# Attention backward on one core: which unit of a group hands a product to GpSimd, and where turned dK, dV and dQ are placed

## The chip, the cores and the metric

The kernel runs on one NeuronCore of a Trainium2 chip. The core has five engines with their own instruction queues: TensorE (PE, with weight loads shown as PEld), VectorE (DVE), ScalarE (ACT), GpSimd (POOL) and SyncE (SP, which issues DMAs). Every queue is worked off in order; engines wait for each other on semaphores. The metric is the device time of one execution in microseconds (us), taken as the median over several runs.

## The reference

The reference is one transformer layer with adaptive layer norm, forward and backward: 2048 tokens of width 512, 32 heads of width 16, and a squared-ReLU MLP of width 1792. It returns the layer's output and the gradients of all inputs but one. What matters here is the backward pass through the attention:

```python
scores = jnp.einsum('bhqd,bhkd->bhqk', q, k) * scale
p = _softmax(scores, axis=-1)
o = jnp.einsum('bhqk,bhkd->bhqd', p, v)
...
_out, _vjp = jax.vjp(_f, A_x, A_wqkv, A_wo, B_w1, B_b1, B_w2, B_b2, c, w_mod)
_grads = _vjp(grad_out)
```

With P = exp(scores), unnormalised, and dO already divided by the softmax sums, the backward pass is: dP = dO V^T minus the row term, dS = P * dP, dV = P^T dO, dK = dS^T Q, dQ = dS K. The row term rides along in two extra rows of the matmul that makes dP, so the only elementwise work on a tile of dP is one product with P.

## The kernel before

The kernel has three parts in time: the forward pass with the MLP forward and backward mixed into it (to about 1172 us), the attention backward loop `attn_bwd` (to about 2416 us), and a last part with the weight gradients of the projection and the gradient of x. The change lies in `attn_bwd` alone.

**Loops.** The 32 heads are taken two at a time: 8 quads `g` times 2 pairs `jp` give 16 passes, called pairs here. Within a pair, `c` runs over 4 chunks of 512 keys and `ib` over 16 blocks of 128 queries. One (c, ib) is a unit: a tile of 128 queries by 512 keys for both heads of the pair (`a` = 0, 1). There are 1024 units. Four units with neighbouring `ib` form a group; a pair has 16 groups, numbered here 0 to 15 as `4*c + ib//4`. Within a group the unit's number is `i`.

**A step.** For each unit the loop body issues, in program order:

1. at `i == 2`, one waiting entry of `turnq`, if there is one (line 1578; see below);
2. for each head: the score matmul of this unit (L1584, into a tile of the PSUM pool `stp`), the matmul dP of the unit before (L1509, in `dP`, into a tile of the PSUM pool `dpp`) with its product dS = dP * P on VectorE (L1513), and then exp on ScalarE (L1587), which writes P into `pu`;
3. the entry of the unit before into the lists `pend` and, at the end of a group, the DMA transpose of the group's dS from SP (L1530, in `dS`);
4. in odd steps the matmuls of dK and dV for two earlier units (`kv_two`, L1455), in even steps those of dQ from dS transposed two to three groups earlier (`dq`, L1478);
5. at `i == 2`, `turn_ds`.

So the product of unit i falls in step i + 1: step 1 of a group makes dP and dS of unit 0, step 2 those of unit 1, and unit 3 is finished in step 0 of the next group. The two pools `stp` and `dpp` have three buffers each, so a matmul into either waits until the tile three places earlier has been read. The score and dP matmuls of a head use different halves of the array's rows and run side by side.

**Two kinds of groups.** `off(c, ib)` is true for the groups with odd numbers. In these, called thinned groups here, one of VectorE's eight products is left out: for unit 0, head 1, `dP` returns the tile, and `dP_pool` has ScalarE copy it to an SBUF tile (L1521, `junk6` or `csq` in turn) and GpSimd multiply it with P (L1522). The call stands after the exponential of head 1 in the same step. All 32 blocks of these groups' dS are transposed by DMA. In the even groups VectorE makes all eight products, and `turn_ds` transposes 4 of the 32 blocks on TensorE (L1543), which ScalarE copies out (L1544); the DMA transposes the other 28.

**dK, dV and dQ.** dK and dV of a chunk gather in one PSUM bank over 16 units; after the last of them, which falls in step 3 of the next even group, ScalarE copies the bank to `kvT` (L1458). These are [rows of the head, keys] and must be turned: `turn` transposes 8 blocks on TensorE (L1468) into a tile of `stp`, and ScalarE copies the parts out (L1472, two copies). A pair's dQ gathers in `accq`, is scaled by VectorE into `dqT` (L1483), and turned by `turn_q` (four transposes, L1491; one copy, L1492). Finished pieces wait in `turnq`, and one is taken per group. In 15 of the 16 pairs, groups 1 and 2 turn halves of the pair before's dK and dV, and group 3 turns its dQ.

**Order.** The order on TensorE, SP and GpSimd is that of the program in this loop. ScalarE and VectorE are ordered by the framework's planner; in the trace their order in this loop is that of the program too. GpSimd also issues the loads of the next pair's operands (L1573), each after a one-element copy (`tick`, L1572) that ties it to the product of unit 0, head 0 of the group before.

Of the kernel before, what the change touches and what calls it, by code (L numbers as in the profile page):

```python
# [105 lines left out]
class K:  # L106
# [1322 lines left out]
    def attn_bwd(self):  # L1429
# [17 lines left out]
        pend, pendq, turnq = [], [], []  # L1447
# [12 lines left out]
        def turn(g, jp, kvT, s0):  # L1460

            if kvT is None:
                return turn_q(g, jp)
            h0 = 4 * g + 2 * jp
            n = ST // 2
            tp = stp.tile([P, n, P], BF16, name="st")
            for st in range(n):
                nc.tensor.transpose(tp[:, st, :], kvT[:, (s0 + st) * P:(s0 + st + 1) * P], self.ident[:])  # L1468
            v = tp[:].rearrange("p s (t a e) -> p t s a e", t=2, a=2)
            for t, dst in enumerate((self.dk_t, self.dv_t)):  # L1470
                d = dst[:, s0:s0 + n, h0 * DH:(h0 + 2) * DH].rearrange("p s (a d) -> p s a d", a=2)
                nc.scalar.copy(d, v[:, t, :, :, 0:DH])  # L1472

        def dq(u):
            (T, g, jp, c, ib0, a, sub, dsT) = u
            col = 32 * (2 * jp + a) - DH * a
            for i in range(G):
                nc.tensor.matmul(accq[32 * i:32 * i + 32, ib0 // G, :], lhsT=T["K"][:, 4 * c + sub, col:col + 32],  # L1478
                                 rhs=dsT[:, (i * 2 + a) * 4 + sub, :],
                                 start=(c == 0 and ib0 == 0 and a == 0 and sub == 0), stop=False,  # L1480
                                 skip_group_check=True)
            if (c, ib0, a, sub) == (SC - 1, ST - G, 1, 3):
                nc.vector.tensor_scalar(self.dqT[:], accq[:].rearrange("p b q -> p (b q)"), self.scale, None, ALU.mult)  # L1483
                turnq.append((g, jp, None, 0))
# [9 lines left out]
        def kv_two(n=2):  # L1494
            for u in pend[2 - n:2]:
                kv(u)
            (T, g, jp, c, ib, kvT, pu, ds) = pend[1]
            del pend[:2]
            if c % 2 and ib == ST - 1 and (g, jp) == (NQ - 1, 1):
                turnq.append((g, jp, kvT, 4 * (c - 1)))  # L1500
            elif c == SC - 1 and ib == ST - 1:
                turnq.extend((g, jp, kvT, s0) for s0 in (0, ST // 2))

        def dP(u, a):

            (T, g, jp, c, ib, kvT, pu, dsg, i, grp) = u
            rd = slice(64 - 64 * jp, 128 - 64 * jp)
            dp = dpp.tile([P, 512], F32, name="dp")
            nc.tensor.matmul(dp[:], lhsT=T["dOT"][rd, ib * P:(ib + 1) * P],  # L1509
                             rhs=masked["VT"][a][rd, 512 * c:512 * (c + 1)], start=True, stop=True)  # L1510
            if a == 1 and i == 0 and off(c, ib):
                return dp
            nc.vector.tensor_tensor(dsg[:, i, a], dp[:], pu[:, a, :], ALU.mult)  # L1513

        def off(c, ib):
            return (c * SC + ib // G) % 2 == 1

        def dP_pool(u, dp):
            (T, g, jp, c, ib, kvT, pu, dsg, i, grp) = u
            f = (self.junk6, self.csq)[(c * SC + ib // G) // 2 % 2]  # L1520
            nc.scalar.copy(f[:], dp[:])  # L1521
            nc.gpsimd.tensor_tensor(dsg[:, i, 1], f[:], pu[:, 1, :], ALU.mult)  # L1522

        def dS(u):

            (T, g, jp, c, ib, kvT, pu, dsg, i, grp) = u
            pend.append((T, g, jp, c, ib, kvT, pu, dsg[:, i]))
            if i == G - 1:
                dsT, n = grp
                nc.sync.dma_start_transpose(dsT[:, n:, :], dsg[:].rearrange("p i a k -> p (i a k)")[:, n * P:])  # L1530
                for a in range(2):
                    for sub in range(4):
                        pendq.append((T, g, jp, c, ib - G + 1, a, sub, dsT))

        def turn_ds(dsg, grp, skip):

            dsT = dtp.tile([P, 8 * G, P], BF16, name="dsT")
            grp.extend((dsT, 0 if skip else 4))
            if skip:
                return  # L1540
            tp = stp.tile([P, 4, P], BF16, name="st")
            for b in range(4):
                nc.tensor.transpose(tp[:, b, :], dsg[:, 0, 0, b * P:(b + 1) * P], self.ident[:])  # L1543
            nc.scalar.copy(dsT[:, 0:4, :], tp[:])  # L1544
# [4 lines left out]
        for g in range(NQ):  # L1549
            for jp in range(2):  # L1550
                if jp == 0:
                    if g + 1 < NQ:
                        Tn, later = self.load_group(g + 1)
                    else:
                        Tn, later = None, self.wq_pieces(1) + self.load_wmt()
                    cut = len(later) // 2 if Tn else len(later)
                    pieces = self.pair_pieces(g, 1) + later[:cut]
                    later = later[cut:]
                elif g + 1 < NQ:
                    pieces = self.pair_pieces(g + 1, 0) + later  # L1560
                else:
                    pieces = [(self.xhat1_6[:, st, :], self.xhat1_d.rearrange("(st p) d -> p st d", p=P)[:, st, :])
                              for st in range(ST)]
                kvT = kvp.tile([P, S], BF16, name="kvT")
                total = len(pieces)
                for c in range(SC):
                    c0 = 512 * c
                    for ib0 in range(0, ST, G):
                        m = c * (ST // G) + ib0 // G
                        while pieces and (total - len(pieces)) * SC * ST <= m * G * total:  # L1570
                            if last:
                                nc.gpsimd.tensor_copy(tick[:], last[7][0:1, 0, 0, 0:1])  # L1572
                            nc.gpsimd.dma_start(*pieces.pop(0))  # L1573
                        dsg, grp = self.dsp.tile([P, G, 2, 512], BF16, name="ds"), []
                        for i in range(G):
                            ib = ib0 + i
                            q = slice(ib * P, (ib + 1) * P)
                            if turnq and i == 2:
                                turn(*turnq.pop(0))
                            pu = self.pup.tile([P, 2, 512], BF16, name="pu")  # L1580
                            for a in range(2):
                                stt = stp.tile([P, 512], F32, name="st")
                                rs = slice(64 * jp, 64 * jp + 64)
                                nc.tensor.matmul(stt[:], lhsT=T["QT"][rs, q], rhs=masked["KT"][a][rs, c0:c0 + 512],  # L1584
                                                 start=True, stop=True)
                                held = dP(last, a) if last else None
                                nc.scalar.activation(pu[:, a, :], stt[:], ACT.Exp, scale=self.scale)  # L1587
                                if held is not None:
                                    dP_pool(last, held)
                            if last:  # L1590
                                dS(last)
                            last = (T, g, jp, c, ib, kvT, pu, dsg, i, grp)
                            if i % 2 == 1 and len(pend) >= 4:
                                kv_two()
                            elif i % 2 == 0 and len(pendq) > 4 * G:
                                for _ in range(8 if len(pendq) > 6 * G else 4):
                                    dq(pendq.pop(0))
                            if i == 2:
                                turn_ds(dsg, grp, off(c, ib))
            T = Tn  # L1600
# [341 lines left out]
```

## Time and profile before

| | |
|---|---|
| median of 3 runs | 2537.41 us (2536.33 to 2538.63) |
| profiled execution, its own time | 2543.74 us |
| its span, first to last instruction | 2542.0 us |
| TensorE clock granted, mean | 0.995 |
| busy in the span: PE, DVE, ACT, POOL | 2439.2, 1694.4, 2297.5, 714.1 us |
| busy in 1250 to 2400 us (1150 us): PE, DVE, ACT, POOL | 1105.73, 1087.48, 1119.30, 293.30 us |
| product on VectorE (L1513), mean of one | 680 ns |
| exp on ScalarE (L1587), mean of one | 646 ns |
| product on GpSimd (L1522), mean of one | 1153 ns |
| DMA transpose of dS, issue to landing (L1530), median | 7.5 us |

A line of the costliest groups reads: source line, engine, operation, tile written <- tiles read, shape, count | busy us, mean ns of one | idle us of the engine just before, and what released it. A row of the time order reads: start in us, duration in us, engine, source line, operation, tiles, count, and in brackets the idle time before it with its releaser; neighbouring instructions of the same kind are merged into one row. A row of the waits reads: who waited <- whom: us in total, times, longest. A row of busy times reads: stretch, length, then busy us and count for PE, PEld, DVE, ACT and POOL, the granted clock, the DMA share and GB/s. Busy times of PE and ACT overlap from one instruction to the next, so a high share alone does not tell that an engine has no room.

### The profile page before, as it was taken

What the parts mean: (1) busy time and instruction counts of PE and PEld (TensorE: products, weight loads), DVE (VectorE), ACT (ScalarE), POOL (GpSimd) and SP (SyncE); (2) the same over time, 40 slices, a digit from 0 to 9 for tenths busy, and PEclk for the clock granted to TensorE, in tenths of its full rate; (3) what the DMA queues carried; (4) which work ended last, traced back from release to release, by engine and by line L of the source; (5) the groups of instructions that cost most, each with busy time, mean ns of one, the idle gap of its engine ahead of it and who ended that gap; (6) DMA issues with size and microseconds to landing.
All of it is one profiled execution on the core that took longest, in us unless ns stands there. A gap on an engine that the chain in (4) does not pass through costs nothing.

```text
span 2542.0 us, 76903 instructions
## 1 busy us (share of the span) xinstructions
PE 2439.2 (96%) x30791; PEld 1108.4 (44%) x30791; DVE 1694.4 (67%) x3519; ACT 2297.5 (90%) x3773; POOL 714.1 (28%) x1289
## 2 busy tenths in 40 slices
PE   8999999999999999999999999999999999999998
PEld 4555555555555554663333333333333333333343
DVE  6222223422332343677999999999999999999957
ACT  7999999999999997435999999999999999999945
POOL 2344521320131031354222222222222222222223
PEclk9999999999999999999999999999999999999999
DMA  4589652440351053799999999999999999999996
GB/s 165 133 184 210 169 106 80 103 109 30 107 134 50 22 159 105 160 190 212 224 220 216 213 218 220 223 223 217 216 216 220 220 219 217 217 226 235 231 221 181
DMA packets 1260558, 446.30 MB, mean 176 GB/s; under 512 B 1204052, under 2 KB 1228246, under 8 KB 1260198
## 3 DMA queue, kind: packets, MB, share of 16 engines
q1 hardware_dynamic: 1219654, 336.29, 70.5%
q0 software_dynamic: 38464, 104.04, 13.9%
q8 instruction: 241, 3.95, 0.7%
q10 hardware_dynamic: 2080, 1.05, 0.1%
q14 instruction: 119, 0.97, 0.1%
HBM read 75.83 MB, written 64.49 MB: 55 GB/s over the span
## 4 chain that ended last, share of the span: by engine, by line
PE 55%; ACT 26%; DMA 12%; issue 4%; DVE 2%; POOL 0%; SPq 0%; DVEq 0%; ACTq 0%; POOLq 0%
ACT pu L391 17%; PE st L1584 14%; DMA dsT<-ds 9%; PE st L388 8%; PE acckv L1455 7%; ACT pu L1587 7%; PE accq L1478 4%; PE accbank L322 3%; PE dp L1509 3%; PE dps L1050 2%; PE pps L1237 2%; PE dp L1635 2%; PE dps L995 1%; PE st L1543 1%; PE pps L631 1%
## 5 line engine op out<-in xcount | busy, mean ns | idle before, releaser
L1513 DVE TENSOR_TENSOR ds<-dp,pu 128x512 bf16<-128x512 f32 x1920 | 1168.3, 680 | 68.8 <-PE dp L1509 52.3
L1587 ACT ACTIVATE pu<-st 128x512 bf16<-128x512 f32 x2048 | 1077.5, 646 | 53.0 <-PE st L1584 21.3
L391 ACT ACTIVATE pu<-st 128x1024 bf16<-128x1024 f32 x992 | 912.3, 1077 | 4.6 <-PE st L388 4.4
L388 PE MATMUL st<-QTm,KTq 128*128 128x512 bf16 x1984 | 588.6, 377 | 19.7 <-ACT pu L391 6.0
L322 PEld LDWEIGHTS <-pu 128*128 128x128 bf16 x8192 | 347.1, 96 | 236.4 <-issue 3.5
L322 PE MATMUL accbank<-Vaug,pu 128*128 128x17 bf16 x8192 | 357.5, 171 | 1.2 <-ACT Vaug L522 0.9
L1509 PE MATMUL dp<-kvm,q 64*128 64x512 bf16 x1024 | 356.5, 383 | 1.3 <-DVE g2w L1056 0.7
L1509 PE MATMUL dp<-kvm,dOTg 64*128 64x512 bf16 x1024 | 354.9, 381 | 0.0
L1584 PE MATMUL st<-kvm,QTg 64*128 64x512 bf16 x1024 | 326.4, 380 | 17.4 <-ACT pu L1587 10.0
L1584 PE MATMUL st<-kvm,q 64*128 64x512 bf16 x1024 | 327.2, 382 | 15.7 <-ACT pu L1587 9.1
L388 PEld LDWEIGHTS <-KTq 128*128 128x128 bf16 x1984 | 188.3, 96 | 177.4 <-issue 125.5
L1522 POOL TENSOR_TENSOR ds<-junk,pu 128x512 bf16<-128x512 f32 x64 | 73.8, 1153 | 311.5 <-ACT junk L1521 311.5
L302 POOL DMA_DIRECT2D QTm<-QTq_d x124 | 63.5, 514 | 342.7 <-PE st L388 321.3
L1455 PE MATMUL acckv<-ds,q 128*16 128x512 bf16 x1024 | 154.5, 382 | 0.0
L1455 PE MATMUL acckv<-pu,q 128*16 128x512 bf16 x1024 | 154.5, 382 | 0.0
L1455 PE MATMUL acckv<-ds,Qg 128*16 128x512 bf16 x1024 | 154.4, 381 | 0.0
L1455 PE MATMUL acckv<-pu,dOg 128*16 128x512 bf16 x1024 | 154.0, 381 | 0.0
L1522 POOL TENSOR_TENSOR ds<-csq,pu 128x512 bf16<-128x512 f32 x64 | 73.8, 1153 | 277.8 <-ACT csq L1521 277.8
L329 DVE RECIPROCAL rl<-accbank 128x4 f32<-128x4 f32 x128 | 22.9, 179 | 159.1 <-PE accbank L322 158.8
L1572 POOL COPY tick<-ds 1x1 bf16<-1x1 bf16 x251 | 44.3, 176 | 297.3 <-DVE ds L1513 297.2
L1584 PEld LDWEIGHTS <-q 64*128 64x128 bf16 x1024 | 60.5, 94 | 134.5 <-issue 102.5
L1584 PEld LDWEIGHTS <-QTg 64*128 64x128 bf16 x1024 | 60.2, 94 | 132.2 <-issue 98.9
(387 smaller groups left out, 3189.0 us busy)
## 6 DMA issues: line engine op xcount, KB each, us to landing
KTq<-KTq_d POOLq DMA_DIRECT2D x24, 512.0 KB, 3.9
duT_d<-auT POOLq DMA_DIRECT2D x3, 1792.0 KB, 8.0
aT_d<-rT POOLq DMA_DIRECT2D x3, 1792.0 KB, 11.7
KTq_d<-KTq SPq DMA_DIRECT2D x32, 128.0 KB, 2.1
QTq_d<-ev_fm SPq DMA_DIRECT2D x32, 128.0 KB, 4.2
ktm_d<-ev_tm POOLq DMA_DIRECT2D x32, 128.0 KB, 2.5
VTq_d<-vT POOLq DMA_DIRECT2D x4, 1024.0 KB, 6.7
dsT<-ds SPq DMA_TRANSPOSE x256, 7.5
```

Source lines behind the costliest of these rows:

```text
L302: nc.gpsimd.dma_start(QTm[j][32 * j:32 * j + 32, :], self.QTq_d[g, 32 * j:32 * j + 32, 512 * qc:512 * (qc + 1)])
L322: nc.tensor.matmul(acc[:, a, sub, :], lhsT=pu[:, a, sub * P:(sub + 1) * P], rhs=Vaug[:, kb, h, :], start=(kb == 0 and a == 0 and sub == 0) ...
L388: nc.tensor.matmul(stt[:, a, :], lhsT=KT[:, kb * P:(kb + 1) * P], rhs=QTm[2 * jp + a][:], start=True, stop=True)
L391: nc.scalar.activation(pu[:], stt[:], ACT.Exp, scale=self.scale)
L1050: nc.tensor.matmul(pt[:], lhsT=a[st], rhs=g_tm[:, st, :], start=(st == 0), stop=(st == ST - 1))
L1455: nc.tensor.matmul(acckv[r:r + DH, :], lhsT=T[n][:, ib, col:col + DH], rhs=src[:, a, :], start=(ib == 0), stop=(ib == ST - 1))
L1478: nc.tensor.matmul(accq[32 * i:32 * i + 32, ib0 // G, :], lhsT=T["K"][:, 4 * c + sub, col:col + 32], rhs=dsT[:, (i * 2 + a) * 4 + sub, :], ...
L1509: nc.tensor.matmul(dp[:], lhsT=T["dOT"][rd, ib * P:(ib + 1) * P], rhs=masked["VT"][a][rd, 512 * c:512 * (c + 1)], start=True, stop=True)
L1513: nc.vector.tensor_tensor(dsg[:, i, a], dp[:], pu[:, a, :], ALU.mult)
L1522: nc.gpsimd.tensor_tensor(dsg[:, i, 1], f[:], pu[:, 1, :], ALU.mult)
L1584: nc.tensor.matmul(stt[:], lhsT=T["QT"][rs, q], rhs=masked["KT"][a][rs, c0:c0 + 512], start=True, stop=True)
L1587: nc.scalar.activation(pu[:, a, :], stt[:], ACT.Exp, scale=self.scale)
```

## The change

Two conditions in `attn_bwd` change. In thinned groups the tile that goes by way of ScalarE to GpSimd is that of unit 1, head 1, not of unit 0, head 1: it is made, copied and multiplied in step 2 of the group, not in step 1. And an entry of `turnq` is turned at the head of step 1 of a group, not of step 2. The number of instructions of every kind stays as it is.

```diff
@@ dP
                              rhs=masked["VT"][a][rd, 512 * c:512 * (c + 1)], start=True, stop=True)
-            if a == 1 and i == 0 and off(c, ib):
+            if a == 1 and i == 1 and off(c, ib):
                 return dp
             nc.vector.tensor_tensor(dsg[:, i, a], dp[:], pu[:, a, :], ALU.mult)
@@ attn_bwd
                             q = slice(ib * P, (ib + 1) * P)
-                            if turnq and i == 2:
+                            if turnq and i == 1:
                                 turn(*turnq.pop(0))
```

One more line depends on the unit's number and isn't changed. In `dP_pool`, GpSimd writes `dsg[:, i, 1]`, with the `i` of the unit itself, so the product lands in unit 1's place after the change.

## The prediction

> **What bounds the kernel now.** I read the page's costliest groups first, then the busy time of the loop's steady stretch, its list of waits, and one pair of heads in time order on VectorE, TensorE and ScalarE. The edit touches only the attention backward loop, about 1172 to 2416 us. I call "step i" what the loop issues for unit i of a group: the scores of unit i, but dP and dS of the unit before. So the product left out for unit 0 falls in step 1, and the change moves it to step 2.
>
> ```profile
> L1513 DVE TENSOR_TENSOR ds<-dp,pu 128x512 bf16<-128x512 f32 x1920 | 1168.3, 680 | 68.8 <-PE dp L1509 52.3
> L1522 POOL TENSOR_TENSOR ds<-junk,pu 128x512 bf16<-128x512 f32 x64 | 73.8, 1153 | 311.5 <-ACT junk L1521 311.5
> ...
> 1250.00:2400.00 1150.00, 1105.73 (x15920) 387.03 (x15917) 1087.48 (x1790) 1119.30 (x2266) 293.30 (x589) 1.00 1.17 220
> ...
> DVE ds L1513 <- PE dp L1509: 46.1, 123, 1.4
> DVE ds L1513 <- ACT junk L1521: 13.8, 14, 1.1
> PE st L1584 <- ACT pu L1587: 18.4, 52, 0.4
> PE accq L1478 <- DMA dsT<-ds: 11.5, 27, 1.3
> ```
>
> VectorE idles 62 of 1150 us, nearly once per thinned group (120 in this stretch). ScalarE shows 1119 busy, but its records overlap (below). In time order, VectorE's idle time before a row is in brackets:
>
> ```profile
> 1570.81 4.87 DVE L1513 TENSOR_TENSOR ds<-dp,pu 128x512 bf16<-128x512 f32 x8 [0.84 <-PE dp L1509]
> 1575.87 1.29 DVE L1513 TENSOR_TENSOR ds<-dp,pu 128x512 bf16<-128x512 f32 x2 [0.19 <-PE dp L1509]
> 1581.30 9.06 DVE L1513 TENSOR_TENSOR ds<-dp,pu 128x512 bf16<-128x512 f32 x15 [0.56 <-PE dp L1509]
> 1600.15 9.20 DVE L1513 TENSOR_TENSOR ds<-dp,pu 128x512 bf16<-128x512 f32 x15 [0.23 <-PE dp L1509]
> 1609.66 9.12 DVE L1513 TENSOR_TENSOR ds<-dp,pu 128x512 bf16<-128x512 f32 x15 [0.31 <-PE dp L1509]
> ```
>
> Between gaps VectorE runs 15 products without a break, one every (9.06 - 0.68)/14 = 0.60. Each gap of the 15-runs stands right after the product left to GpSimd. The TensorE rows around the last one:
>
> ```profile
> 1608.27 0.37 PE L1584 MATMUL st<-kvm,q 64*128 64x512 bf16 x1 [0.20 <-ACT pu L1587]
> 1608.28 0.39 PE L1509 MATMUL dp<-kvm,q 64*128 64x512 bf16 x1
> 1608.59 0.39 PE L1455 MATMUL acckv<-ds,q 128*16 128x512 bf16 x2
> ...
> 1609.14 0.39 PE L1509 MATMUL dp<-kvm,q 64*128 64x512 bf16 x1
> ...
> 1609.40 0.37 PE L1509 MATMUL dp<-kvm,q 64*128 64x512 bf16 x1
> 1609.71 0.41 PE L1478 MATMUL accq<-dsT,keep 128*32 128x128 bf16 x16
> 1610.05 0.39 PE L1584 MATMUL st<-kvm,q 64*128 64x512 bf16 x1
> 1610.22 0.37 PE L1509 MATMUL dp<-kvm,q 64*128 64x512 bf16 x1
> ```
>
> From a step's second dP to the next step's first: 1609.14 - 1608.28 = 0.86 across the dK/dV matmuls (odd steps), 1610.05 - 1609.40 = 0.65 across the dQ matmuls (even steps). From dP to its product: 1609.66 - 1609.14 = 0.52.
>
> **The gap in numbers.** dP has three PSUM buffers, so a second dP issues when the product three tiles back has ended: T = that product's start + 0.73 (0.68 and a hop of 0.05). VectorE's slots then reach to T + 0.47, T + 1.07, and T + 1.67 where no product is left out. The next product can start at T + 0.86 + 0.52 = T + 1.38 (dK/dV between) or T + 1.17 (dQ between). With all products there, 1.67 covers both. With one left out in step 1, 1.38 - 1.07 = 0.31; less the 0.08 by which records overlap, 0.23 idle: the row at 1600.15. With a turned dQ (0.33, from 1580.44 to 1580.77) between: 0.64, shown 0.56 at 1581.30. With a turned dK/dV (0.55, from 1569.73 to 1570.28): 0.86, 0.78 shown, against 0.84. In an unthinned group the same turn after dK/dV: 1.93 - 1.67 = 0.26, 0.18 shown, against 0.19 at 1575.87. So one sum explains the gaps.
>
> **The skill.** The Trainium skill, Perfetto Trace Analysis, Optimization Strategy, says that a gap repeating on the engine that should be saturated can mean too few SBUF/PSUM buffers for the next tile. The trace agrees: the dP buffers set T. GPSIMD Engine Reference, Specifications, gives GpSimd no PSUM access, hence the ScalarE copy ahead; GpSimd's product waits for it (311.5 us). SBUF — State Buffer, Who interferes with whom, lets a VectorE tensor-tensor contend with GpSimd only with both inputs in SBUF. Here one is in PSUM; the 15-runs with GpSimd's product inside keep 0.60 each.
>
> **The change, part by part.** Nothing is added or removed: as many copies, products, transposes and DMAs.
>
> (a) *Left-out product in step 2.* Behind it stands dQ, not dK/dV: gap 1.17 - 1.07 = 0.10. But the next step's second dP again has only two products ahead: its T' is 0.73 after the start of unit 1's first product, slots reach T' + 1.17 (they shift by the 0.10), dK/dV gives 1.38: 0.21. Sum 0.31, as before: an ordinary cycle of two groups gains 0 (48 of them).
>
> (b) *Cycles with a kvT copy in the unthinned group* (three per pair without turns). The copy holds ScalarE 0.56 (1607.01 to 1607.57), so TensorE's second scores of step 1 wait for an exponential (0.20 above), delaying dP. Today that lands where only two products cover it: 0.31 and 0.45 shown at 1609.66 and 1590.81, about 0.54 mean by following all such cycles through the trace. Afterwards a third product (0.60) covers the 0.20, and the gap falls to 0.31 to 0.35: gain 0.2, times 3 = 0.6 per pair.
>
> (c) *Turns at the head of step 1*, behind dQ of step 0: in group 1, 0.65 + 0.55 + 0.52 = 1.72 against 1.67: 0.05, plus the ordinary 0.31, in place of 0.86: gain 0.50. Group 2: 0.05 in place of 0.26: 0.21. Group 3: 0.65 + 0.33 + 0.52 = 1.50, covered, and 0.31 in place of 0.64: 0.33. Sum 1.04 per pair.
>
> ```profile
> 1570.05 0.59 ACT L1521 COPY junk<-dp 128x512 f32<-128x512 f32 x1
> 1570.51 0.41 ACT L1472 COPY dk_t<-st 128x256 bf16<-128x256 bf16 x1
> ...
> 1571.04 4.09 ACT L1587 ACTIVATE pu<-st 128x512 bf16<-128x512 f32 x8
> ```
>
> Today the dP copy (0.46) and the turn's copies (0.53) stand back to back on ScalarE; afterwards two units' exponentials lie between. But the turn's copies then precede the exponentials of step 1, right after the kvT copy, and leave ScalarE some 0.4 behind at the end of group 1, which group 2's turn takes up. I charge 0.3 per pair, and 0.1 for late landings.
>
> Sum: 0.6 + 1.04 - 0.4 = 1.24 per pair, times 15.5 (turns in 15 pairs) = 19 us. The profiled execution, 2543.7 (span 2542.0), would go to 2524.7; the runs' median lies 6 lower, so 2537.4 - 19 = **2518**.
>
> At nothing, with their cover: GpSimd's product comes one step, about 1.2 us, later. The group's DMA transpose on SP waits for VectorE's last product anyway, two units further, more than 1 us after GpSimd's end. dK/dV of that unit comes three steps after its dP rather than two. Queued behind it on GpSimd are a tick (0.18) and one piece's DMA (0.57), needed a pair or more later. Were the cover gone, SP would hold the transpose and dQ would wait. The turned dQ comes a step sooner after VectorE's scaling to dqT, whose slot ends three steps ahead.
>
> **Rivals.** *ScalarE is the bound*, and gaps closed on VectorE reopen there. For: 1119 of 1150. Against: four exponentials take 2.12, so one starts every 0.49; two cycles need 32 x 0.49 + 2 x 0.46 + 2 x 0.47 (dsT) + 0.56 = 18.1 against some 19.0 now. It allows most of the 19, unless waits between spoil it: a gain of 4, 2533.
>
> *DMA transposes land late.* dQ waits 11.5 us in 27 places; a faster loop leaves less time to land. Doubled, it takes back 11: 2529.
>
> *Slower: the copy frees its dP buffer late.* Three tiles after the held one, the next dP waits for ScalarE's copy: 1610.22 stands 0.17 behind its scores at 1610.05 (and 13.8 us in 14 waits). Moved, that dP stands after dK/dV at the next group's step 0, where only two products cover it. By my sum the copy ends 0.1 to 0.3 before it is needed; if it came 0.25 too late in all 128 groups, 32 us are lost and 13 remain after the 19: 2550. It decides from 0.15.
>
> *More:* if the charge of 0.4 doesn't fall due, and the copy's 13.8 us of waits go too: 19 + 6 + 10: 2502.
>
> **Chances.** Forecast (2508 to 2528) 0.50, more 0.08, late DMA 0.10, ScalarE 0.12, slower 0.20. About 0.2%, 5 us, is what a measurement of this kernel can tell from no change: faster 0.68 (forecast, more, late DMA), same 0.12, slower 0.20. The range 2502 to 2546 leaves out about half of the slower case and of "more".
>
> **What would show it.** VectorE's waits for dP fall from 46 to about 30 us; the single gap after the left-out product becomes two small ones (0.02 and 0.13 idle in ordinary cycles); the 0.84, 0.56 and 0.19 of the turns shrink; the list of ScalarE's work reads copy, exponentials, turn, apart. Wrong: waits of VectorE on the copies above 30 us, ScalarE idle unchanged with VectorE idle moved elsewhere, or dQ waiting for dsT in many more than 27 places.

## The result

| | before | after |
|---|---|---|
| median | 2539.14 us (6 runs, 2536.33 to 2549.12) | 2523.72 us (6 runs, 2520.55 to 2526.96) |
| ratio, 95% interval | | 0.9935 (0.9922 to 0.9948) |
| profiled span | 2542.0 us | 2522.4 us |
| attention backward loop, first to last score matmul of a unit | 1243.6 us | 1229.4 us |

The kernel before was measured again beside the changed one. The change is faster by 0.65%: 16.5 us of 2539, between 13 and 20. In the profiled executions the loop is 14.3 us shorter. The other 5 us between the spans lie ahead of the loop and behind it, where the code is the same; they are a difference between two executions, not a gain.

From the costliest groups of the changed kernel:

```profile
L1513 DVE TENSOR_TENSOR ds<-dp,pu 128x512 bf16<-128x512 f32 x1920 | 1178.3, 681 | 44.5 <-PE dp L1509 26.4
```

Its busy times in 1250 to 2400 us (length, then PE, PEld, DVE, ACT, POOL, then clock, DMA share and GB/s):

```profile
1250.00:2400.00 1150.00, 1116.59 (x16093) 392.00 (x16091) 1109.16 (x1810) 1130.19 (x2292) 295.65 (x594) 1.00 1.17 223
```

Its waits in the same stretch:

```profile
DVE ds L1513 <- PE dp L1509: 23.7, 58, 1.6
PE st L1584 <- ACT pu L1587: 13.9, 41, 0.5
PE accq L1478 <- DMA dsT<-ds: 11.2, 20, 1.6
```

VectorE's waits for dP halve, from 46.1 us to 23.7. Its waits of 13.8 us for ScalarE's copy of dP are gone from the list. ScalarE is busier than before (1130 against 1119 of 1150): the same work in less time.

VectorE in time order over one pair (the bracket is the idle time before the row):

```profile
1561.36 4.60 DVE L1513 TENSOR_TENSOR ds<-dp,pu 128x512 bf16<-128x512 f32 x7 [0.63 <-PE dp L1509]
1566.22 2.48 DVE L1513 TENSOR_TENSOR ds<-dp,pu 128x512 bf16<-128x512 f32 x4 [0.26 <-PE dp L1509]
1568.62 0.68 DVE L1483 TENSOR_SCALAR dqT<-accq 128x512 bf16<-128x512 f32 x1
1569.22 61.30 DVE L1513 TENSOR_TENSOR ds<-dp,pu 128x512 bf16<-128x512 f32 x99
```

Before, a gap stood after every 15 products. Now 99 run in one row, (61.30 - 0.68)/98 = 0.619 each against 0.60 without any gap: what is left is too short to part the row. The two gaps that remain are those of the turns, 0.63 in group 1 and 0.26 in group 2.

The loop is best read by two groups at a time. I followed all pairs but the first through both traces and summed how much later than 0.605 us after the one before each product starts (the slot of the dqT scaling taken off, products that start earlier counted as nothing). The mean in us per two groups:

| groups of a pair | before | after | change |
|---|---|---|---|
| 0 and 1 (kvT copy, turn) | 1.20 | 0.85 | -0.35 |
| 2 and 3 (turn, turned dQ) | 0.91 | 0.92 | +0.01 |
| 4, 8, 12 and the next (kvT copy) | 0.66 | 0.37 | -0.29, three times |
| 6, 10, 14 and the next (ordinary) | 0.37 | 0.46 | +0.09, three times |

Sum: -0.35 + 0.01 + 3 x (-0.29 + 0.09) = -0.94 per pair; times 15.5, 14.6 us, beside the 14.3 by which the loop is shorter. Gaps given as averages below are of this kind.

One execution is not exact to a few us. A second profiled execution of the change (taken beside two later kernels) has a loop of 1236.3 us, 7 longer. Its four rows are 0.78, 0.96, 0.35 and 0.63. So the gains of the first and third row recur; the loss of the fourth varies, most of it in a few long waits of dQ for transposes (two of 2.1 and 2.4 us in groups 14).

### The profile page after: what moved, and what is told of

It is laid out like the page before. It is cut to its first block, busy times and chain, and to the rows that moved or that the text cites. A ratio compares the mean times of both kernels' runs of the same rounds, so it can differ in the third digit from the quotient of the medians.

```text
span 2522.4 us, 76903 instructions
## 1 busy us (share of the span) xinstructions
PE 2433.1 (96%) x30791; PEld 1107.9 (44%) x30791; DVE 1705.4 (68%) x3519; ACT 2296.2 (91%) x3773; POOL 713.9 (28%) x1289
## 4 chain that ended last, share of the span: by engine, by line
PE 59%; ACT 22%; DMA 11%; issue 4%; DVE 3%; SPq 1%; POOL 0%; DVEq 0%; ACTq 0%; POOLq 0%
ACT pu L391 18%; PE st L1584 17%; DMA dsT<-ds 8%; PE acckv L1455 8%; PE st L388 8%; PE accq L1478 5%; PE accbank L322 3%; PE dp L1509 3%; ACT pu L1587 2%; PE dps L1050 2%; PE pps L1237 2%; PE dps L995 1%; DVE ds L1513 1%; PE st L1543 1%; PE pps L631 1%
## 5 line engine op out<-in xcount | busy, mean ns | idle before, releaser
L1584 PEld LDWEIGHTS <-q 64*128 64x128 bf16 x1024 | 58.1, 94 | 137.9 <-issue 104.5
L1509 PEld LDWEIGHTS <-q 64*128 64x128 bf16 x1024 | 88.4, 93 | 64.2 <-issue 47.4
```

## The experiments

Unless said otherwise, a kernel differs from the change only by its diff, and times are medians with the ratio to the kernel before on the same chip.

**The product moved alone.**

```diff
-                            if turnq and i == 1:
+                            if turnq and i == 2:
```

> The product of unit 1 goes to GpSimd, turns stay at step 2. My sum of gaps: 0.6 per pair from the cycles with a kvT copy; group 1 then has 0.26 + 0.31 of gap in place of 0.86, group 3 has 0.04 + 0.31 in place of 0.64, group 2 is as before; together 1.18 per pair, 18 us, and ScalarE gets its copies further apart, so no charge: about 2521, the change's own time or slightly less. Rival, that the turns' place carries the gain: at most 8 us, 2531.

2532.64 us, ratio 0.9953 (0.9938 to 0.9969): 12 us by the ratio, between 8 and 16 by its interval, and 8 by the medians. That is less than my 18, and the rival's "at most 8" lies at its edge. In the traces, cycles with a kvT copy go from 0.66 to 0.46 (0.37 in the change). The turn's gap in group 2 did not stay at 0.26, as I had it, but grew to 0.42.

**The turns moved alone.**

```diff
-            if a == 1 and i == 1 and off(c, ib):
+            if a == 1 and i == 0 and off(c, ib):
```

> Turns at step 1, the product of unit 0 to GpSimd as before. My sum of gaps gives 1.04 per pair for VectorE, but in group 1 the copies of kvT, of the turn and of dP now follow each other closely on ScalarE, which in the profile of the change already costs most of it: I expect 0 to 0.4 per pair, 2533 to 2539. Rival, that VectorE's gaps alone count: 1.04 x 15.5 = 16 us, 2523.

2537.76 us, ratio 0.9984 (0.9976 to 0.9993): 4 us, as the charge for ScalarE had it, and far from the 16 of VectorE's gaps alone. So the product carries most of the gain. By the ratios 12 and 4 make the 16.5 of the change; that the parts add up is not shown more closely, for in the one profiled execution of each the loop is 5.5 us shorter than before with the product alone and 2.4 longer with the turns alone. With the product kept at unit 0, the gap after it stays as it was, with and without a kvT copy. VectorE in time order:

```profile
1586.15 9.12 DVE L1513 TENSOR_TENSOR ds<-dp,pu 128x512 bf16<-128x512 f32 x15 [0.45 <-PE dp L1509]
1595.49 9.20 DVE L1513 TENSOR_TENSOR ds<-dp,pu 128x512 bf16<-128x512 f32 x15 [0.23 <-PE dp L1509]
```

**Unit 2 in place of unit 1.**

```diff
-            if a == 1 and i == 1 and off(c, ib):
+            if a == 1 and i == 2 and off(c, ib):
```

> As the change, but unit 2's product goes to GpSimd, in step 3, so dK/dV stands behind it again. Theory (the two gaps of a left-out product sum to 0.31 wherever it stands, and distance from the kvT copy is what gained): gaps of 0.31 and about 0, sum as in the change, so 2520 to 2526, worse only by transposes that start later since GpSimd ends last: dQ's waits for dsT rise from 11 us. Rival (dQ behind the left-out product is what gained): the gain of the ordinary part is lost, 2532 to 2538.

2542.43 us, ratio 1.0007 (0.9997 to 1.0018): the gain is lost, and the time misses my forecast. By time alone the rival would have won. The trace says otherwise. VectorE in time order, in a stretch where dQ does not wait:

```profile
1607.19 9.06 DVE L1513 TENSOR_TENSOR ds<-dp,pu 128x512 bf16<-128x512 f32 x15 [0.23 <-PE dp L1509]
1616.47 9.06 DVE L1513 TENSOR_TENSOR ds<-dp,pu 128x512 bf16<-128x512 f32 x15 [0.23 <-PE dp L1509]
1625.76 9.06 DVE L1513 TENSOR_TENSOR ds<-dp,pu 128x512 bf16<-128x512 f32 x15 [0.23 <-PE dp L1509]
```

The waits of this kernel in 1250 to 2400 us:

```profile
PE accq L1478 <- DMA dsT<-ds: 31.2, 48, 2.8
...
DVE ds L1513 <- POOL ds L1522: 4.4, 13, 0.4
```

With dK/dV behind the left-out product there is one gap of 0.23 idle again, but two groups here take 9.29 (1616.47 to 1625.76), with a kvT copy or without. In the change they take 61.30 / 99 x 15 = 9.29 too. So the sum of a left-out product's gaps is the same in either place, and the distance from the kvT copy is kept. What was lost is on the DMA: dQ waits 31.2 us for transposed dS, 20 more than in the change, and the loop is 1249.4 us long, 20 more. In the trace, VectorE's gap after the dQ of a group's step 0 averages 0.60 where that dQ waited and 0.00 where it didn't. GpSimd's product starts only some 0.4 us ahead of the group's last product on VectorE, and so mostly ends last: half of these groups issue their transpose 0.96 us or more after the start of VectorE's last product, where 0.74 is usual. The added waits are for these groups' transposes: in the whole loop dQ waits over 0.1 us for a thinned group in 50 places (21 in the change), for an even one in 8 (4 in the change). A kernel with this unit and later dQ was not tried.

**Turns later.**

```diff
-                            if turnq and i == 1:
+                            if turnq and i == 1 and m not in (0, 1, 4):
```

> As the change, but turns are taken in groups 2, 3 and 5 of a pair, not 1, 2 and 3, so that none follows the kvT copy in group 0. Theory (ScalarE behind after the kvT copy costs the turn's gain): 0.3 to 0.5 per pair faster than the change, 5 to 8 us, 2516 to 2519, and the gap in group 2 (0.55 idle in the change) falls below 0.2. Rival (the turn itself costs that wherever it stands): as the change, 2524.

2532.16 us, ratio 0.9956 (0.9939 to 0.9972): not faster than the change, against the forecast 5 to 8 us. Half of the theory held: in groups 0 and 1 the gaps fall from 0.85 to 0.33. But the turn that now falls into group 2 costs 0.74, though no kvT copy precedes it, and dQ's turn in group 5, right after a kvT copy, costs 0.40. So two things make a turn dear. Over the kernels, the gap at the turn in group 2 (in the kernel with odd groups, below, group 3) goes with the steps since the last left-out product. The last column tells how far TensorE is behind there: how much later than T, 0.73 us after the start of the product three tiles back, it starts the second dP of the step ahead of the turn (median).

| kernel | steps between | mean gap, us | median gap | second dP later than T |
|---|---|---|---|---|
| turns in odd groups, group 3 | 7 | 0.15 | 0.15 | 0.00 |
| before | 5 | 0.26 | 0.26 | 0.01 |
| turns moved alone | 4 | 0.30 | 0.31 | 0.28 |
| product moved alone | 4 | 0.42 | 0.42 | 0.27 |
| the change | 3 | 0.63 | 0.61 | 0.50 |
| turns later | 3 | 0.74 | 0.51 | 0.44 |

TensorE's lag is nearly the same at the same distance. The gap also depends on what stands beside the turn: dK/dV in the kernel before and with the product moved alone, dQ in the others. Group 3 is moreover a thinned group itself.

**Turns in odd groups only**, so that the last left-out product lies 7 steps back.

```diff
-                            if turnq and i == 1:
+                            if turnq and i == 1 and m % 2 == 1:
```

> As the change, but turns are taken only in odd groups: 1, 3 and 5 of a pair. The runs so far let me form a new theory: a turn costs VectorE 0.4 to 0.7 when it comes within 3 or 4 steps after a left-out product (group 2 after group 1), because TensorE has not yet regained its lead. In odd groups the last left-out product lies 7 steps back. Expected: the gap of about 0.63 in group 2 goes, groups 3 and 5 show less than 0.15 at the turn, 0.45 per pair or 7 us faster than the change: ratio to before 0.990 to 0.992. Rival (a turn costs this wherever it stands, or ScalarE's lag after the kvT copy is what counts): no better than the change, 0.9935 or above.

2523.59 us, ratio 0.9957 (0.9944 to 0.9971), not the 0.990 to 0.992 forecast, and the loop is as long as the change's, 1229.4. The gap in group 2 is gone as forecast (0.63 to 0.04), and group 3 shows 0.15. But group 5, where dQ is turned, shows 0.40, and takes the gain back. VectorE in one pair:

```profile
1558.33 6.99 DVE L1513 TENSOR_TENSOR ds<-dp,pu 128x512 bf16<-128x512 f32 x11 [0.63 <-PE dp L1509]
1565.23 0.68 DVE L1483 TENSOR_SCALAR dqT<-accq 128x512 bf16<-128x512 f32 x1
1565.83 11.93 DVE L1513 TENSOR_TENSOR ds<-dp,pu 128x512 bf16<-128x512 f32 x19
1578.09 1.96 DVE L1513 TENSOR_TENSOR ds<-dp,pu 128x512 bf16<-128x512 f32 x3 [0.32 <-ACT pu L1587]
```

No gap in group 2 (inside the first row), but 0.32 idle at 1578.09, and it is ScalarE's exponential that VectorE waits for there. So distance isn't all: the kvT copy, ahead of those exponentials on ScalarE, may count too. The next kernel tests that.

**The same with dQ in group 7.**

```diff
-                            if turnq and i == 1:
+                            if turnq and i == 1 and m in (1, 3, 7, 11):
```

> As the change, but turns are taken in groups 1, 3 and 7 of a pair (in the last pair in 11 too). It differs from the turns in groups 1, 3 and 5 only in dQ's place, which no longer follows a kvT copy. If a turn in the group after a kvT copy costs 0.4 because ScalarE is behind there, group 5's gap of 0.43 goes and 0.15 at most comes in group 7: 0.3 per pair, 4 us faster than turns in 1, 3 and 5 and than the change. Rival (only the distance to the left-out product counts): as with groups 1, 3 and 5.

2520.63 us, ratio 0.9925 (0.9912 to 0.9937), beside the change on the same chip at 0.9939 (0.9924 to 0.9953). The gaps of the cycles with a kvT copy fall back from 0.52 to 0.40. The 0.40 in group 5 (0.43 in the forecast) is gone, and the same turn costs 0.03 in group 7, at the same distance of 7 steps: being close to the kvT copy is what made it dear. In time the step from the change is 2 us by the medians, where 4 were forecast, and not resolved.

**All turns away from both.** The first half of dK and dV is turned in its own pair.

```diff
-            if c % 2 and ib == ST - 1 and (g, jp) == (NQ - 1, 1):
+            if c % 2 and ib == ST - 1:
-                            if turnq and i == 1:
+                            if turnq and i == 1 and m % 4 == 3:
```

> As the change, but the first half of dK and dV is turned in group 11 of its own pair (its chunks are finished by then), the second half in group 3 of the next pair, dQ in group 7: every turn in an odd group and without a kvT copy in the group before. The theory of distance and the charge for ScalarE both say that about 0.5 (group 1) and 0.55 (group 2) of gap per pair go: 1.0 x 15.5 = 15 us faster than the change, 2508 beside 2524. If only distance counts, as for turns in groups 1, 3 and 5. Rival (turns cost the same anywhere): as the change.

2518.39 us, ratio 0.9933 (0.9921 to 0.9946); once more, beside the change:

> The kernel with turns in groups 11, 3 and 7 once more, beside the change on the same chip: by the loop's gaps 5 us faster than the change, ratio to before 0.003 lower or 0.002; rival: no difference, the earlier one having come from one execution.

> The change itself once more, beside the next two on the same chip: ratio to before 0.992 to 0.995 by every theory.

2520.28 us, ratio 0.9921 (0.9903 to 0.9939), against 2522.27 and 0.9939 (0.9924 to 0.9953) for the change. The 15 us forecast did not come. In the two profiled executions of each the loop is 1224.7 and 1230.6 us long, in the change 1229.4 and 1236.3: some 5 us shorter on average, no more than the difference between two executions of one kernel. By the runs it is at best slightly faster. In groups 0 and 1 the gaps fall to 0.34, in 2 and 3 to 0.56, but the turns leave 0.15, 0.03 and 0.25 in their new places (groups 3, 7 and 11), where my sum had 0.05 for a turned dK/dV and none for dQ, and dQ still waits at times. It beats the kernel before clearly; whether it beats the change stays open.

**No product left out.** GpSimd multiplies nothing and ScalarE copies no dP; otherwise as the change.

```diff
-            if a == 1 and i == 1 and off(c, ib):
+            if a == 1 and i == 9 and off(c, ib):
```

> As the change, but no product is left out: VectorE makes all sixteen of two groups, ScalarE makes no copy of dP, GpSimd multiplies nothing. The sum of gaps says that the gaps in cycles without turns vanish and VectorE's 16 x 0.60 = 9.6 per two groups is the bound, against 15 x 0.60 + 0.35 = 9.35 of the change: 0.2 to 0.25 x 128 = 26 to 32 us slower than the change, about 2552, with VectorE's waits for dP below 10 us. Rival (a left-out product is worth its full 0.60): 77 us slower, 2600.

2561.41 us, ratio 1.0103 (1.0085 to 1.0122); the loop is 37 us longer than the change's. The waits in 1250 to 2400 us:

```profile
ACT pu L1587 <- PE dp L1509: 63.6, 188, 3.3
...
DVE ds L1513 <- PE dp L1509: 11.7, 19, 3.0
```

VectorE hardly waits for dP any more, and ScalarE waits for TensorE instead. In ordinary cycles the gaps fall from 0.46 to 0.16, in those with a kvT copy from 0.37 to 0.12. So leaving a product out opens its gap, and of the 0.60 x 128 = 77 us that it takes off VectorE, about half is lost again. I had put the loss at 26 to 32 us, near the measured 37; the gaps of the turns, which mostly stay (0.74 in groups 0 and 1), I had left out.

**Four buffers for dP, two for the scores.**

```diff
-        self.stp = self.open_pool("p5st", bufs=3, space=PSUM)
-        self.dpp = self.open_pool("p5dp", bufs=3, space=PSUM)
+        self.stp = self.open_pool("p5st", bufs=2, space=PSUM)
+        self.dpp = self.open_pool("p5dp", bufs=4, space=PSUM)
```

> As the change, but dP has four PSUM buffers and the scores (with the turned tiles) two. If three dP buffers are what opens the gap after a left-out product, that gap goes, while scores now wait for exponentials: each two scores cost ScalarE about 2 x 0.56 rather than 2 x 0.49, some 10.2 per two groups in place of 9.6, 2580 to 2610, with TensorE waiting for ScalarE in most steps. Rival (TensorE's order alone sets the gap): the gap stays beside it.

2683.77 us, ratio 1.0586 (1.0567 to 1.0605), worse than forecast. VectorE waits for dP 39.8 us in 153 places and for exponentials 55.3 us in 199. Waits for exponentials, with only two score buffers, now hide whatever the fourth dP buffer does, and so this run tells nothing on the gap with more dP buffers. That three of them set T shows in the trace of the kernel before: no second dP starts sooner than 0.73 us after the product three tiles back, and 53% start between 0.73 and 0.76. That a fourth would close the gap is not shown.

## Why the prediction was right, and where it wasn't

**(a) The left-out product in step 2, forecast 0.** Measured +0.09 per ordinary cycle. From the trace, the two gaps are 0.10 and 0.24, where the sum had 0.10 and 0.21; the rest is 0.1 at step 0's dQ, which waits now and then for transposes (more in the second execution, 0.63 - 0.37 = 0.26 in all). The gaps were right; for the waits only 0.1 per pair stood in the charge of (c). The run with unit 2 shows that it is not dQ behind the product that helps.

**(b) Cycles with a kvT copy, forecast 0.2.** Measured 0.29. The gap came down to 0.37, where I had 0.31 to 0.35. Right in mechanism and nearly in size.

**(c) The turns, forecast 1.04 less a charge of 0.4, so 0.64.** Measured 0.34, all of it in groups 0 and 1; groups 2 and 3 gained nothing. This is the step that failed, in its line for group 2: "0.05 in place of 0.26". It became 0.63, which cancels group 3's gain. The sum took each second dP to issue when VectorE frees its buffer (T). The rows of the changed kernel in group 2:

```profile
1563.30 0.37 PE L1509 MATMUL dp<-kvm,q 64*128 64x512 bf16 x1
...
1564.15 0.39 PE L1509 MATMUL dp<-kvm,q 64*128 64x512 bf16 x1
...
1564.39 0.39 PE L1509 MATMUL dp<-kvm,q 64*128 64x512 bf16 x1
1564.70 0.41 PE L1478 MATMUL accq<-dsT,keep 128*32 128x128 bf16 x16
1565.04 0.62 PE L1468 MATMUL st<-ident,kvT 128*128 128x128 bf16 x8
1565.60 0.39 PE L1509 MATMUL dp<-kvm,q 64*128 64x512 bf16 x1
...
1566.22 1.29 DVE L1513 TENSOR_TENSOR ds<-dp,pu 128x512 bf16<-128x512 f32 x2 [0.26 <-PE dp L1509]
```

From 1563.30 on, TensorE waits for nobody: 0.85 for dK/dV, 0.24 to the second dP, 1.21 for dQ and the turn, 0.62 to the product, 2.92 in all. The seven products before it began at 1561.36 and fill slots to 1561.36 + 7 x 0.60 = 1565.56, or 0.3 later with the gaps of the left-out product. VectorE has been catching up on TensorE ever since that product, three steps back, and TensorE has no lead to spend on a turn. This pair is a mild one. In 11 of the 15 pairs the second score matmul of step 0 also waits 0.12 to 0.13 for an exponential.

The traces give the size of the miss. Ahead of group 2's turn, the second dP starts at T before the change (0.73 to 0.74 after the product three tiles back in 14 of 15 pairs), but 1.11 to 1.24 after it in the change, in the median 0.50 later than T. And from dP to its product it takes 0.62 behind a turn in step 1, where the sum had 0.52. Then 0.05 + 0.50 + 0.10 = 0.65, against a median gap of 0.61. Before the change five steps lay between product and turn, and TensorE's lead had come back. Moving the product one step later and the turn one step earlier brought them two steps closer.

Group 1 fell short too. The 0.86 that I took for its turn before is one pair's; over all pairs it is 1.07.

**The charge for ScalarE** was real. The moved turn follows the kvT copy closely; here is ScalarE in the changed kernel:

```profile
1559.13 0.73 ACT L1458 ACTIVATE kvT<-acckv,kvs 128x512 bf16<-128x512 f32 x1
1559.70 1.14 ACT L1587 ACTIVATE pu<-st 128x512 bf16<-128x512 f32 x2
1560.65 0.45 ACT L1472 COPY dk_t<-st 128x256 bf16<-128x256 bf16 x1
1560.90 0.47 ACT L1472 COPY dv_t<-st 128x256 bf16<-128x256 bf16 x1
1561.17 2.18 ACT L1587 ACTIVATE pu<-st 128x512 bf16<-128x512 f32 x4
1563.14 0.68 ACT L1521 COPY junk<-dp 128x512 f32<-128x512 f32 x1
```

The gap at the turn is 0.42 in group 1 of the change, right after a kvT copy, but 0.15 at the same kind of turn in group 3 of the run with odd groups. For dQ's turn it is 0.40 in group 5, after a kvT copy, and 0.03 in group 7, without one. My sum had 0.05 for group 1, and the charge lay in group 2. The order of the copies came out as said: copy of dP and turn are apart.

**The rivals.** A late copy of dP did not come: its waits went from 13.8 us to none in the list. Late transposes stayed about as they were in the change (11.5 us before, 11.2 and 14.1 in its two executions), but the run with unit 2 shows how little it takes: with an issue some 0.2 us later in the middle case, dQ waited 20 us more and the whole gain was gone. ScalarE as the bound of this change fell: with 1119 of 1150 busy before, it now does more work in the same stretch (1130), and the loop gained. Whether it limits further gains is not shown.

The end, 2518 forecast against 2523.7, is right in sign and within the range; 19 us became 16.5. The sum 1.24 per pair was 0.94, with (a) and (b) off by 0.0 net and (c) short by 0.3. That (a) and (b) cancel is luck: (a) lost 0.27 per pair where 0 was forecast, (b) gained 0.27 more than forecast.

## What to carry to other kernels

Work taken off the pacing engine can pay less than its length when its producer has few buffers: here half of it came back as a gap, and which matmuls stand behind decided only how the gap is split. Extra work on the producer (a turn) was cheapest far from such a place, and far from extra work on the engine that frees the producer's other buffers; count the steps between, not only the work within a step. In this kernel the gaps show that, while the time that it gained beyond the change was not resolved. When an experiment's time speaks for a rival, look where its gaps are: a late transfer can hide that the mechanism under test was right.

## What the runs showed of the hardware

Records of neighbouring instructions overlap: VectorE's products last 0.68 us and start every 0.60, ScalarE's exponentials last 0.65 and start every 0.49 (four in 2.12 us). So ScalarE at 1119 us of 1150 had room for the same work in less time. GpSimd's product, 1.15 us long, hardly slowed VectorE's products beside it: in runs without a gap they start every 0.60 us without it, and every 0.60 (before) to 0.61 (the change) beside it.
